# Moving split projection matmuls to later chunks, and the instruction-page edge by 8 instructions

## Chip, cores and metric

One core of a Trainium2 chip runs the whole program. The metric is the device time of one execution in microseconds (us). Times of single instructions are in nanoseconds (ns) where that is said.

## What is computed

The reference runs two blocks, twice each in turn, on x of 2048 tokens by 512 channels, with a layer norm before each and a residual added after each:

```python
for s in range(n_seg):                       # 64 segments of 32 tokens
    h = concat([mem, xs])                    # 8 memory tokens + 32 tokens
    q, k, v = h @ Wq, h @ Wk, h @ Wv         # 32 heads of 128
    p = softmax(mask(q k^T * scale))
    o = (p v) @ Wo                           # back to 512 channels
    mem = o[:, :M]                           # the next segment's memory
    outs.append(o[:, M:])
```

That is block A, a recurrence: the first 8 output rows of a segment are the memory of the next. Block B projects with w_in, applies gelu, normalises one half, multiplies it by the 2048 x 2048 matrix w_sp, gates the other half with it and projects with w_out. It has no recurrence.

## The kernel before, in words

`a_block` (L479) runs block A, `b_block` (L227) block B; the program is A, B, A, B. All weights of A stay in SBUF. In A the loop at L837 goes over 64 segments and calls `segment` (L681). PE, VectorE and ScalarE get their instructions in the order in which the code writes them (`tc.manual_schedule`), so the order in `segment` is the order on TensorE.

A segment's work on TensorE, in order:
- `qk(0)`, `qk(2)`, `qk(1)`, `qk(3)` (L695): the projections q0, k0, q1, k1, each for 16 heads, into `psm`. They need `hA`, the segment's 32 rows transposed, which `build_hA` (L651) makes once the output pass of the segment before has given the new memory.
- `scores(0)` (L712), then `v_mm(0)` (L705, the value projection v0 into `psV`), a `fill()`, `scores(1)`, `v_mm(1)` (v1), a `fill()`.
- the sums psM (L785), `pv` (L737), the sums psD (L791), a `fill()`.
- the output pass `wo_pass` (L595) into `pw`: 32 heads times 4 column groups, 128 matmuls of 128 columns, and a last `fill()`.

A fill takes the next piece of `more`, a generator. For s % 4 of 1 to 3 it is `b_units` (L570), the projections of the last 8 tokens of all segments of the next block of 128 tokens, which don't depend on the recurrence; for s % 4 == 0 from the fifth block of 128 on it is `y_part` (L615), a quarter of the outputs of those tokens.

Each projection of a segment is a chunk made by `mm_chunk` (L530): 4 k-steps times 4 column groups, 16 matmuls of 512 columns with 32 stationary columns each. With `halved=n`, n of the 16 are split into two matmuls of 256 columns each, which compute the same. Every matmul is two instructions on TensorE, a weight load and the matmul, so each split adds two instructions.

What the splits are for is seen in the constants. `PE_PAGE` is 256 instructions. `fills_of(s)` (L663) gives the number of instructions in each of a segment's four fills, SEGMENT_PE (600) what the rest of a segment has, and `pads_of(s)` (L671) the number n of splits that bring the distance from one output pass to the next to 3 x 256 instructions, and how they are dealt out to the chunks. So a multiple of 256 instructions lies at the same place in every segment of a block. `FILL_AHEAD` (L29) stands for the fills ahead of the first segment, one entry for each of the two runs of block A; it enters n of segment 0 alone, and so sets where that place is.

The chunks' splits before, from `pads_of` (each chunk has 16 at most):

| segments | n | q0 | k0 | q1 | k1 | v0 | v1 |
|---|---|---|---|---|---|---|---|
| 0 of the first A, of the second A | 35, 37 | 0 | 0 | 16 | 16 | 3, 5 | 0 |
| s % 4 == 0 or 1, s < 16 (not 0) | 68 | 4 | 16 | 16 | 16 | 16 | 0 |
| s % 4 == 0 or 1, 16 to 60 | 64 | 0 | 16 | 16 | 16 | 16 | 0 |
| s % 4 == 2 or 3, to 59 | 52 | 0 | 4 | 16 | 16 | 16 | 0 |
| 61 | 80 | 16 | 16 | 16 | 16 | 16 | 0 |
| 62, 63 | 84 | 16 | 16 | 16 | 16 | 16 | 4 |

Of the kernel before, what the change touches and what calls it, by code (L numbers as in the profile page):

```python
# [25 lines left out]
LN_EXP_SET = 6  # L26
PE_PAGE = 256
SEGMENT_PE = 600
FILL_AHEAD = ((0, 0, 0, 98), (0, 0, 0, 94))  # L29
FCH = [(0, 128), (128, 128), (256, 128), (384, 128), (512, 128), (640, 48)]  # L30
ORDERED = {mybir.EngineType.PE, mybir.EngineType.DVE, mybir.EngineType.Activation}

# [446 lines left out]
def a_block(tc, c, rows, front, MV_in, RS_in, MV_out, RS_out, wqkv, Wo, S, first):  # L479
# [6 lines left out]
    with ExitStack() as ctx:  # L486
# [176 lines left out]
        def fills_of(s):  # L663

            if s < 0:
                return FILL_AHEAD[not first]
            if s % 4 == 0:
                return (2, 2, 4, 8) if s // 4 > 3 else (0, 0, 0, 0)
            return (8, 8, 16, 32) if s // 4 + 1 < NB else (0, 0, 0, 0)

        def pads_of(s):  # L671

            n = (3 * PE_PAGE - SEGMENT_PE - fills_of(s - 1)[3] - sum(fills_of(s)[:3]) + 1) // 2
            pads = {}
            for chunk in ("q1", "k1", "v0", "k0", "q0", "v1"):
                pads[chunk] = min(n, 16)
                n -= pads[chunk]
            assert n == 0
            return pads

        def segment(s, fill, spare1, spare2, tail):  # L681
            tb, j4 = s // 4, s % 4
            pads = pads_of(s)
            st = seg_state.pop(s)
            QQ, KTB, VB = st["QQ"], st["KTB"], st["VB"]
# [239 lines left out]
```

## Time and profile before

| | before |
|---|---|
| median of 6 executions | 1861.03 us |
| lowest to highest | 1854.25 to 1865.81 us |
| the profiled execution, its own time | 1859.94 us |
| its span in the profile | 1858.2 us |
| TensorE matmuls busy | 1758.0 us, 51180 of them |
| weight loads busy | 1225.7 us, 51180 |
| VectorE busy | 1155.1 us |
| ScalarE busy | 1112.2 us |
| matmuls psm with Wk, at L544 | 281.1 us, 7440 of them, mean 285 ns |
| matmuls psV with Wv, at L544 | 274.1 us, 6136, mean 310 ns |
| matmuls pw at L599 | 258.8 us, 16640, mean 220 ns |
| mean granted TensorE clock | 0.988 |

The page gives busy time and share of the span for each engine, then DMA queues, then the chain: from the last instruction back, at each step to what released it. "Issue" in the chain is time in which an engine waited for nothing that the profile shows. A mean time of one matmul is the time that it is in the array's pipe, not the time that it adds[...]. What a chunk adds is read from start to start in the timeline. In a row of the chain of waits stand the start and the length in us, then the engine, the written tile, the line and the number of instructions merged.

### The profile page before, as it was taken

To read this page: it belongs to the slowest core of one execution; us is meant where nothing else is said; L and a number is where in the kernel's file an instruction comes from. 1 tells how busy PE (TensorE), PEld (TensorE's weight loads), DVE (VectorE), ACT (ScalarE), POOL (GpSimd) and SP (SyncE) were. 2 spreads that over 40 slices of the span, in tenths; PEclk is the share of its full clock that TensorE was granted. 3 is DMA by queue.
4 is the path that set the end of the run, shared out by engine and by line. 5 is a ranking of instruction groups with operands and counts; after the bars stand their busy time and mean duration, and the time that the engine had idled before them with its cause. 6 is when DMAs were issued, how large, how long until landed. Compare 5 with 4: busy or idle time off the path is not lost.

```text
span 1858.2 us, 109480 instructions
## 1 busy us (share of the span) xinstructions
PE 1758.0 (95%) x51180; PEld 1225.7 (66%) x51180; DVE 1155.1 (62%) x2700; ACT 1112.2 (60%) x2074; POOL 136.7 (7%) x289
## 2 busy tenths in 40 slices
PE   2999999999999999888989999999999999998898
PEld 1677777777777777645547777776677767765455
DVE  1666666676667766583346666666766676665722
ACT  1667766777777676571037767666677666665500
POOL 5000000000000000122010000000000000002000
PEclk8999999999999999999989999999999999999999
DMA  9100000021002111359840000001200120124585
GB/s 348 51 19 21 19 21 19 21 74 38 19 19 81 35 31 34 100 144 182 197 125 22 23 22 23 23 22 44 81 25 22 49 84 26 35 62 145 113 177 131
DMA packets 189327, 126.78 MB, mean 68 GB/s; under 512 B 135896, under 2 KB 164328, under 8 KB 188872
## 3 DMA queue, kind: packets, MB, share of 16 engines
q1 hardware_dynamic: 167016, 71.01, 16.2%
q0 software_dynamic: 10560, 34.07, 5.6%
q10 hardware_dynamic: 11296, 14.70, 2.6%
q8 instruction: 400, 6.55, 1.5%
q14 instruction: 55, 0.45, 0.1%
HBM read 59.29 MB, written 33.56 MB: 50 GB/s over the span
## 4 chain that ended last, share of the span: by engine, by line
PE 88%; DVE 4%; DMA 4%; ACT 2%; issue 2%; POOL 0%; SPq 0%; ACTq 0%; DVEq 0%; POOLq 0%
PE psm L544 25%; PE psV L544 13%; PE pw L599 12%; PE psb L544 10%; PE pg L332 7%; PE psS L720 5%; PE psO L743 4%; PE pwB L611 4%; PE py L360 3%; PE psD L795 2%; PE pz L266 2%; PE psM L785 1%; DMA Wk_sb<-in_A_Wk_dram 1%; DMA uT<-u 1%; PE psM L786 1%
## 5 line engine op out<-in xcount | busy, mean ns | idle before, releaser
L544 PEld LDWEIGHTS <-hA 128*32 128x32 bf16 x19872 | 521.4, 96 | 173.1 <-DVE hA L655 51.3
L699 ACT CAST rows<-psm 128x512 bf16<-128x512 f32 x512 | 300.1, 586 | 211.9 <-PE psm L544 211.9
L544 PE MATMUL psm<-Wk_sb,hA 128*32 128x256 bf16 (+1 forms) x7440 | 281.1, 285 | 8.8 <-issue 8.0
L544 PE MATMUL psm<-Wq_sb,hA 128*32 128x256 bf16 (+1 forms) x6296 | 275.9, 307 | 11.1 <-DVE hA L655 9.8
L544 PE MATMUL psV<-Wv_sb,hA 128*32 128x256 bf16 (+1 forms) x6136 | 274.1, 310 | 2.4 <-issue 2.4
L599 PEld LDWEIGHTS <-uT 128*32 128x32 bf16 x16640 | 234.4, 97 | 54.7 <-DVE uT L805 47.8
L599 PE MATMUL pw<-Wo_sb,uT 128*32 128x128 bf16 x16640 | 258.8, 220 | 11.6 <-DVE uT L805 6.7
L703 DVE STREAM_TRANSPOSE QQ<-rows 128x512 bf16<-128x512 bf16 x256 | 182.1, 711 | 77.3 <-ACT rows L699 76.2
L703 DVE STREAM_TRANSPOSE KA<-rows 128x512 bf16<-128x512 bf16 x256 | 181.9, 711 | 58.3 <-ACT rows L699 58.3
L724 ACT ACTIVATE E<-psS 128x448 bf16<-128x448 f32 x256 | 140.0, 547 | 127.8 <-PE psS L720 127.8
L755 DVE TENSOR_TENSOR uT<-psO,Rt 128x384 bf16<-128x384 f32 x256 | 138.6, 541 | 119.6 <-ACT Rt L811 119.4
L805 DVE TENSOR_TENSOR uT<-psO,Rm 128x128 bf16<-128x128 f32 x256 | 62.6, 286 | 164.6 <-PE psD L795 164.6
L811 ACT ACTIVATE Rt<-Rt 128x512 f32<-128x512 f32 x256 | 157.6, 629 | 4.1
L332 PE MATMUL pg<-z2n,wspT 128*128 128x344 bf16 x1024 | 156.5, 311 | 1.0 <-DVE u L340 1.0
L332 PEld LDWEIGHTS <-wspT 128*128 128x128 bf16 x1024 | 98.5, 98 | 55.6 <-issue 8.2
L803 ACT ACTIVATE Rt<-psD 128x1024 f32<-128x1024 f32 x128 | 131.2, 1025 | 5.9
L544 PEld LDWEIGHTS <-hB 128*32 128x32 bf16 x3072 | 77.6, 97 | 78.2 <-DVE hB L559 24.4
L720 PEld LDWEIGHTS <-KA 128*64 128x64 bf16 x2048 | 80.3, 113 | 68.0 <-DVE KA L703 34.8
L727 DVE TENSOR_TENSOR E<-E,maskN 128x448 bf16<-128x448 bf16 x256 | 95.3, 372 | 47.9 <-ACT E L724 47.9
L544 PE MATMUL psb<-Wq_sb,hB 128*32 128x512 bf16 x1024 | 90.1, 389 | 25.5 <-DVE hB L559 25.5
L720 PE MATMUL psS<-QQ,KA 128*64 128x80 bf16 x2048 | 111.9, 208 | 0.7 <-issue 0.3
L780 ACT CAST VA<-psV 128x512 bf16<-128x512 f32 x128 | 75.1, 586 | 56.6 <-PE psV L544 56.6
(147 smaller groups left out, 2226.0 us busy)
## 6 DMA issues: line engine op xcount, KB each, us to landing
Wo_sb<-in_A_Wo_dram POOLq DMA_DIRECT2D x8, 1024.0 KB, 13.3
xs<-xd ACTq DMA_DIRECT2D x32, 256.0 KB
o_d<-o_sb SPq DMA_DIRECT2D x126, 64.0 KB
y_o<-o_d SPq DMA_DIRECT2D x24, 256.0 KB
xd<-y_o SPq DMA_DIRECT2D x22, 256.0 KB
Wq_sb<-in_A_Wq_dram POOLq DMA_DIRECT2D x8, 512.0 KB, 6.9
Wk_sb<-in_A_Wk_dram POOLq DMA_DIRECT2D x8, 512.0 KB, 11.0
Wv_sb<-in_A_Wv_dram POOLq DMA_DIRECT2D x8, 512.0 KB, 11.2
```

The source lines that it names most:

```text
L332: nc.tensor.matmul(pg[t][:, k, 0:344], lhsT=wsp[t][:, st, :], rhs=z2n[:, st, 344 * k:344 * k + 344], start=(st == 0), stop=(st == NT - 1))
L544: nc.tensor.matmul(o, lhsT=lhs(kt, cg), rhs=r, start=(kt == 0 and a == 0), stop=(kt == KT - 1 or halved > 0), tile_position=(0, 32 * cg), ...
L599: nc.tensor.matmul(po[32 * cg:32 * cg + 32, 0:128], lhsT=lhs[:, n, :], rhs=wo_rhs(h, cg), start=(h == 0), stop=(h == H - 1), tile_position ...
L699: nc.scalar.copy(r[:], ps[:])
L703: nc.vector.transpose(out=QQ[:, j % 2, :, 0:32] if j < 2 else KA[:, j % 2], in_=r[:])
L720: nc.tensor.matmul(pS[64 * g:64 * g + 64, i, c0:80 if K is KA else 112], lhsT=K[:, r, n:n + 2, :].rearrange("p h k -> p (h k)"), rhs=q if ...
L724: nc.scalar.activation(out=E[:, r], in_=pS, func=ACT.Exp, scale=scale)
L727: nc.vector.tensor_tensor(out=E[:, r], in0=E[:, r], in1=maskN[:, j4, :].unsqueeze(1).to_broadcast([P, 4, 112]), op=ALU.mult)
L755: nc.vector.tensor_tensor(out=hview(uT_nxt[:], r, 8, 32), in0=oview(r, 8, 32), in1=Rr[:, :, :, 0:24], op=ALU.mult)
L780: nc.scalar.copy(VA[:, 1].rearrange("p i e -> p (i e)"), psV[1][:, 0, :])
L803: nc.scalar.activation(out=Rt[:], in_=psD[:], func=ACT.Ln)
L811: nc.scalar.activation(out=rt, in_=rt, func=ACT.Exp, scale=-1.0)
```

## The change

Two edits. The first entry of `FILL_AHEAD` goes from 98 to 106, so n of segment 0 in the first A is 31 in place of 35: 8 instructions fewer ahead of everything that follows. And `pads_of` deals the splits out by another list: v0 and k1 first, then v1 (16 for s % 4 == 0, else 8), q1 up to 12, k0 up to 8, and what is left to q1, v1, k0, q0.

```diff
-FILL_AHEAD = ((0, 0, 0, 98), (0, 0, 0, 94))
+FILL_AHEAD = ((0, 0, 0, 106), (0, 0, 0, 94))
...
-            pads = {}
-            for chunk in ("q1", "k1", "v0", "k0", "q0", "v1"):
-                pads[chunk] = min(n, 16)
-                n -= pads[chunk]
+            pads = dict.fromkeys(("q0", "k0", "q1", "k1", "v0", "v1"), 0)
+            for chunk, most in (("v0", 16), ("k1", 16), ("v1", 16 if s % 4 == 0 else 8), ("q1", 12), ("k0", 8), ("q1", 16), ("v1", 16),
+                                ("k0", 16), ("q0", 16)):
+                k = min(n, most - pads[chunk])
+                pads[chunk] += k
+                n -= k
             assert n == 0
             return pads
```

The splits after:

| segments | n | q0 | k0 | q1 | k1 | v0 | v1 |
|---|---|---|---|---|---|---|---|
| 0 of the first A | 31 | 0 | 0 | 0 | 15 | 16 | 0 |
| 0 of the second A | 37 | 0 | 0 | 0 | 16 | 16 | 5 |
| s % 4 == 0, s < 16 (not 0) | 68 | 0 | 8 | 12 | 16 | 16 | 16 |
| s % 4 == 1, s < 16 | 68 | 0 | 8 | 16 | 16 | 16 | 12 |
| s % 4 == 0, 16 to 60 | 64 | 0 | 4 | 12 | 16 | 16 | 16 |
| s % 4 == 1, 16 to 57 | 64 | 0 | 8 | 16 | 16 | 16 | 8 |
| s % 4 == 2 or 3, to 59 | 52 | 0 | 0 | 12 | 16 | 16 | 8 |
| 61 | 80 | 0 | 16 | 16 | 16 | 16 | 16 |
| 62, 63 | 84 | 4 | 16 | 16 | 16 | 16 | 16 |

The total of TensorE's matmuls goes from 51180 to 51176. The other engines and the queues keep their instructions in the same order. The second run of A begins 8 instructions earlier too, so the place of the multiples of 256 moves by 8 instructions in both runs of A: in the output pass, from 96 to 104 instructions after its start in the first A.

## The prediction

> **What bounds the kernel now.** I read the page first.
>
> ```profile
> PE 1758.0 (95%) x51180; PEld 1225.7 (66%) x51180; DVE 1155.1 (62%) x2700; ACT 1112.2 (60%) x2074; POOL 136.7 (7%) x289
> ...
> q8 instruction: 400, 6.55, 1.5%
> ...
> PE 88%; DVE 4%; DMA 4%; ACT 2%; issue 2%; POOL 0%; SPq 0%; ACTq 0%; DVEq 0%; POOLq 0%
> ```
>
> TensorE is the bound: 95% busy and 88% of the chain. The reader is to see two smaller things. Queue q8 carries instructions: 6.55 MB in 400 packets is 16 KB each, and 102,360 PE records (matmuls and weight loads) over 400 is 256 records for each packet. So one packet is one page, and PE_PAGE in the code is its length. 1.5% of 16 engines over 1858.2 us, shared by 400, is 1.11 us for each packet. And 2% of the chain is "issue", time in which PE waited for nothing that the profile shows. Summed over the chain of waits in the six stretches that hold the segments (63 to 780 and 976 to 1708 us), issue is some 21 us. That is about all that a better place for page edges can win.
>
> Next, the chain of waits in a segment with s % 4 == 0 (s = 16 of block 0), from its output pass on:
>
> ```profile
> 223.99 1.80 PE pw L599 x128
> 225.79 0.96 PE psb L544 x16
> 226.75 1.31 PE psm L544 x32
> 228.06 0.33 issue
> 228.39 2.40 PE psm L544 x80
> ...
> 235.82 1.90 PE pw L599 x128
> ```
>
> and TensorE's timeline of the same place:
>
> ```profile
> 226.56 1.05 PE L544 MATMUL psm<-Wq_sb,hA 128*32 128x512 bf16 x16
> 227.43 0.62 PE L544 MATMUL psm<-Wk_sb,hA 128*32 128x256 bf16 x16
> 228.39 0.63 PE L544 MATMUL psm<-Wk_sb,hA 128*32 128x256 bf16 x16 [0.33 <-issue]
> ```
>
> The stall falls inside k0, after 16 of its 32 halves. Nothing in the computation separates those two halves. Counted in instructions (a weight load and a matmul each): 256 of Wo, 32 of fill, 32 of q0, 32 of k0 is 352 = 96 + 256. The segment's other edges lie at 96 and 608. In block 1 the same edge comes one matmul earlier. Its Wo edge shows when pages are late:
>
> ```profile
> 1306.94 0.68 PE pw L599 x47
> 1307.62 0.08 issue
> 1307.70 1.33 PE pw L599 x81
> ...
> 1315.43 0.04 issue
> ...
> 1322.79 0.72 issue
> 1323.50 2.45 PE psm L544 x81
> ```
>
> From 1307.70 to 1323.50 four pages pass in 15.80 us, 3.95 us each, although work alone would take less. So there is a **fetch loop**: while transfers load the engines, a page can't follow the page before in less than 3.9 to 4.0 us. Where the chain shows no issue (the segment from 258.37 to 269.52 us, 11.15 us for three pages), the loop fits in 3.72 us. The kernel runs at the edge of it.
>
> [...] a split is nearly free. Here v0 with 32 halves takes 1.00 us in the chain, v1 with 16 whole ones 0.98.
>
> **The change, part by part.** *Added and removed instructions.* The number of splits is unchanged but for the first segment (35 to 31 in block 0), so 8 instructions fewer: 4 x 0.02/16 us, nothing. Chunks now get 8 or 12 splits, which no row shows. The rows with 4 (k0, 20 matmuls) and 16 start 0.87 and 0.88 us before the next chunk, and bracket them: cost 0. If the two halves of one column group held up the other groups, each k-step would lose 0.11 us, 0.4 us a chunk; 16 splits would then show it worst, and they don't. VectorE, ScalarE, GpSimd and the DMA queues keep their instructions in order; chunks end at the same time, so no evacuation moves.
>
> *The moved edges and splits.* A split chunk spends 13.8 ns on an instruction, a whole one 27, Wo 7. So moving splits changes how long a page lasts. From the on-time chain of a main segment with s % 4 == 0 (1364.85 to 1376.12: Wo 1.80, fill 0.95, q0, k0, q1, k1 3.51 together, scores 0.37, v0 1.00, pwB 0.32, scores 0.37, v1 0.98, pwB 0.32, psM 0.23, pv 0.59, psD 0.29, pwB 0.54):
> - before, pages from 96, 352 and 608: 160/256 x 1.80 + 0.95 + 0.87 + 0.44 = 3.38; then 0.44 + 0.88 + 0.89 + 0.37 + 1.00 = 3.58; then the rest and 96 of Wo, 4.31.
> - after (q0 0, k0 4, q1 12, k1, v0 and v1 16 splits; edges at 104, 360, 616): 1.07 + 0.95 + 0.87 + 0.87 = 3.76; then 0.88 + 0.89 + 0.37 + 1.00 + 0.32 + 0.37 + 0.09 = 3.92; then 3.59.
>
> [...] The timeline's starts of the output pass say what such segments really lose: the 22 main ones take 11.79 us on average and 11.37 at best, 9.1 us in sum; the six early ones 11.57 and 11.14, 2.6 us. So up to 0.4 us a segment could go. [...] I keep half: 22 x 0.2 = 4.4 and 1.3 for the early ones.
>
> *The other segments.* s % 4 of 2 and 3: 3.64, 3.70, 3.81 by the same count from the chain of 258.37; after 3.88, 3.76, 3.51. The sum of 11.15 is under three late loops either way, so they lose the same in busy stretches; I put 0. s % 4 == 1 is similar (third page about 3.4). The last four segments of a block have no fills and are filled with 80 to 84 splits, now with q0 nearly free of them instead of v1: their pieces of issue come to some 6 us, of which I take 0.8.
>
> Sum: 4.4 + 1.3 + 0.8 = 6.5 us. The profiled execution took 1859.94 us (span 1858.2 and 1.7 around it), so 1853.4; it lies 1.1 under the median of 1861.03, and against that median I say **1854.5**. The bounds: nothing (the loop alone decides) and all of 9.1 + 2.6 + about 1.3 = 13 us (1848).
>
> **The rivals.**
> 1. *The loop itself is the bound.* A stall in the busy stretch from 1307.70 is 3L whatever the pages hold. For it: late pages come in runs; against it: issue sits in the s % 4 == 0 segments far more than in the 22 of each of the other kinds (9.1 us lost against 1.8, 2.3 and 4.5 for s % 4 of 1, 2 and 3, counted in the same way). Then only the quiet ones gain, about 1 to 2 us: 1859.
> 2. *The full gain*[...]: 1848.
> 3. *Slower: the third page is now too short.* At 3.4 to 3.5 us instead of 3.7 to 3.8 [...] in the 96 or so segments with s % 4 of 1 to 3. [...] the Wo edge is late by 0.3 us there. It eats the gain of 6.5 us from 22 such stalls on, one segment in four to five; at one in two it costs 48 x 0.3 = 14, net 8 slower: 1869. [...]
> 4. *Unseen serialising in chunks of 8 and 12 splits* would cost far more (0.4 us in some 200 chunks, 80 us), and the chunks of 4 and 16 speak against it.
>
> **How the numbers follow.** Forecast (3 to 9 us won) 0.50; rival 1 0.27; rival 2 0.10; rival 3 0.10; rival 4 0.03. A measurement can tell about 0.3%, 5.6 us, from no change. So faster takes rival 2 and four fifths of the forecast, 0.50; same the rest of the forecast, rival 1 and a fifth of rival 3, 0.39; slower 0.11. The range: 1848 (all of it) to 1863 (rival 1 with the spread of the runs shown, 1854 to 1866, behind it); what is left out is the greater part of rivals 3 and 4.
>
> **What would show it.** Right: in the chain, no issue piece inside k0 of s % 4 == 0 segments, output passes there 11.4 us apart in quiet stretches; in the timeline the k0 chunk with 20 matmuls; q8 again 400 packets. Wrong: pieces of issue inside pw after 52 matmuls, in segments with s % 4 of 1 to 3 (rival 3), or v1 and q1 over 0.95 us from start to next start (rival 4), or the same issue total with its pieces at other places (rival 1).

## The result

| | before | after |
|---|---|---|
| median | 1861.67 us (40 runs, 1853.42 to 1872.82) | 1852.38 us (19 runs, 1844.85 to 1858.59) |
| after over before, 95% interval | | 0.9946 (0.9931 to 0.9960) |
| profiled execution, its own time | 1859.94 us | 1856.67 us |
| its span | 1858.2 us | 1854.9 us |

The change makes the kernel 0.54% faster, with an interval of 0.40 to 0.69%: some 10 us (7 to 13), where 6.5 were forecast. The profiled execution of after is one of its slower ones, so totals are taken from the timed runs, and the profile is used for places.

The page of after, its lines of engines, instruction queue and chain:

```profile
PE 1754.4 (95%) x51176; PEld 1246.3 (67%) x51176; DVE 1156.2 (62%) x2700; ACT 1111.5 (60%) x2074; POOL 136.7 (7%) x289
...
q8 instruction: 400, 6.55, 1.5%
...
PE 86%; DVE 5%; DMA 4%; ACT 2%; issue 2%; POOL 0%; SPq 0%; ACTq 0%; POOLq 0%; DVEq 0%
```

Nothing in these says why one kernel is faster: nearly the same busy times, the same 400 packets, issue at 2% again. The difference is at the page edges. The chain of waits of after in the segment whose chain was shown of before (s = 16 of block 0; start, length, what):

```profile
223.43 1.88 PE pw L599 x128
225.32 0.87 PE psb L544 x16
226.19 1.80 PE psm L544 x24
227.99 0.36 issue
228.35 1.94 PE psm L544 x56
...
235.31 1.72 PE pw L599 x113
```

The stall is still there in this execution, but it has moved. TensorE's timeline shows that it now stands between k0 and q1, where the edge at 360 lies, and that k0 is a chunk of 20 matmuls:

```profile
226.94 1.05 PE L544 MATMUL psm<-Wk_sb,hA 128*32 128x512 bf16 x20
228.35 1.06 PE L544 MATMUL psm<-Wq_sb,hA 128*32 128x512 bf16 x28 [0.36 <-issue]
229.22 1.06 PE L544 MATMUL psm<-Wk_sb,hA 128*32 128x256 bf16 x32
```

So one segment proves little. The gain is in how many segments stall. The table takes each main segment's time from TensorE's timeline, start of one output pass (L599) to the next; a segment that loses nothing takes 11.37, 11.30, 11.15 and 11.15 us for s % 4 of 0, 1, 2 and 3. It has the mean of 22 segments for each kind and the sum of the last four segments of both runs of A. "Again" are the second profiles of both kernels, taken one after the other on one chip.

| profile | 0 | 1 | 2 | 3 | last four, both runs |
|---|---|---|---|---|---|
| before | 11.79 | 11.38 | 11.25 | 11.35 | 97.4 |
| before again | 11.67 | 11.37 | 11.28 | 11.26 | 98.9 |
| after | 11.56 | 11.46 | 11.31 | 11.33 | 97.1 |
| after again | 11.48 | 11.48 | 11.19 | 11.27 | 92.7 |

The same traces say where the time goes. An edge counts as late here when the first matmul behind it starts more than 0.05 us later after the matmul ahead of it than at the best edge of its kind. The first edge is the one in the output pass (96 instructions after its start in before, 104 in after), the second comes 256 instructions later, in k0 or just behind it, and the third another 256 later. The table has the number of late edges in the main segments and what they add up to; an output pass is counted with the segment that follows it.

| late edges | of | before | before again | after | after again |
|---|---|---|---|---|---|
| the second edge, s % 4 == 0 | 22 | 16, 6.8 us | 16, 4.6 us | 8, 3.0 us | 6, 2.0 us |
| the third edge, s % 4 == 0 | 22 | 7, 1.9 us | 8, 1.8 us | 1, 0.2 us | 0 |
| the first edge, all kinds | 88 | 6, 1.3 us | 3, 0.7 us | 24, 5.3 us | 7, 2.3 us |
| the second and third edge, the other kinds | 132 | 22, 5.8 us | 13, 3.6 us | 16, 1.8 us | 2, 0.4 us |

The late edges of the s % 4 == 0 segments sum to 9.0, 6.5, 4.3 and 2.5 us in the four profiles, and that is all that these segments lose against 11.37 us each. The change takes away the late third edge and about half of the lateness at the second, and more edges are late in the output pass.

That these stalls are waits for instructions can be read from the packets on q8, each of which the trace has with its start and end. In before, all 29 stalls of more than 0.15 us at the first and second edge of main segments end 1.24 to 1.61 us after a packet has landed. The packet of the stall at 228.39 us landed at 226.89, that of the stall at 1323.50 at 1322.04.

A pair of chains from those second profiles, of the same segment (s = 36 of block 0), shows the difference of the two deals. Before:

```profile
449.85 1.80 PE pw L599 x128
451.64 0.96 PE psb L544 x16
452.60 1.31 PE psm L544 x32
453.91 0.20 issue
454.11 2.40 PE psm L544 x80
...
461.55 1.45 PE pw L599 x94
```

After:

```profile
448.27 1.80 PE pw L599 x128
450.08 0.95 PE psb L544 x16
451.03 3.49 PE psm L544 x80
...
459.54 1.90 PE pw L599 x128
```

From output pass to output pass it is 11.70 against 11.27 us; with the edge behind k0 and k0 nearly whole, the 1.31 + 0.20 + 2.40 us of the projections become 3.49. The stall costs more than its piece of issue: the first row behind it is 0.2 us longer than the 2.21 us that its chunks take by the prediction's count.

### The profile page after: what moved, and what is told of

It reads as the page before. It is cut to its first block, busy times and chain, and to the rows that moved or that the text cites. A ratio compares the mean times of both kernels' runs of the same rounds, so it can differ in the third digit from the quotient of the medians.

```text
span 1854.9 us, 109472 instructions
## 1 busy us (share of the span) xinstructions
PE 1754.4 (95%) x51176; PEld 1246.3 (67%) x51176; DVE 1156.2 (62%) x2700; ACT 1111.5 (60%) x2074; POOL 136.7 (7%) x289
## 4 chain that ended last, share of the span: by engine, by line
PE 86%; DVE 5%; DMA 4%; ACT 2%; issue 2%; POOL 0%; SPq 0%; ACTq 0%; POOLq 0%; DVEq 0%
PE psm L544 25%; PE psV L544 13%; PE pw L599 12%; PE psb L544 10%; PE pg L332 7%; PE psS L722 5%; PE psO L745 4%; PE pwB L611 3%; PE py L360 3%; PE psD L797 2%; PE psM L787 1%; DMA uT<-u 1%; DMA Wk_sb<-in_A_Wk_dram 1%; PE pz L266 1%; PE psM L788 1%
## 5 line engine op out<-in xcount | busy, mean ns | idle before, releaser
L544 PEld LDWEIGHTS <-hA 128*32 128x32 bf16 x19868 | 542.4, 96 | 171.7 <-DVE hA L655 51.9
L599 PE MATMUL pw<-Wo_sb,uT 128*32 128x128 bf16 x16640 | 263.4, 220 | 16.0 <-DVE uT L807 8.9
L544 PE MATMUL psm<-Wk_sb,hA 128*32 128x256 bf16 (+1 forms) x6623 | 276.1, 299 | 2.5 <-issue 1.7
L599 PEld LDWEIGHTS <-uT 128*32 128x32 bf16 x16640 | 235.8, 97 | 62.6 <-DVE uT L807 50.2
L544 PE MATMUL psV<-Wv_sb,hA 128*32 128x256 bf16 x7477 | 275.3, 284 | 0.9 <-issue 0.9
L544 PEld LDWEIGHTS <-hB 128*32 128x32 bf16 x3072 | 88.8, 98 | 68.0 <-DVE hB L559 24.8
L544 PE MATMUL psb<-Wq_sb,hB 128*32 128x512 bf16 x1024 | 93.9, 397 | 25.9 <-DVE hB L559 25.9
```

The source lines that it names most:

```text
L544: nc.tensor.matmul(o, lhsT=lhs(kt, cg), rhs=r, start=(kt == 0 and a == 0), stop=(kt == KT - 1 or halved > 0), tile_position=(0, 32 * cg), ...
L599: nc.tensor.matmul(po[32 * cg:32 * cg + 32, 0:128], lhsT=lhs[:, n, :], rhs=wo_rhs(h, cg), start=(h == 0), stop=(h == H - 1), tile_position ...
```

## The experiments

Twelve runs were made in three groups, each group on a chip of its own. The chips differ (before has medians of 1850, 1860 and 1849 us in the three), so ratios are compared, each to before on the same chip. A gain in us is the ratio's, times the median of before. The theory is the one of the prediction: pages of 256 instructions against a fetch loop. The rivals keep their numbers; segment times are each from one profile.

**The new deal alone.** The splits as after, the edges as before.

```diff
-FILL_AHEAD = ((0, 0, 0, 106), (0, 0, 0, 94))
+FILL_AHEAD = ((0, 0, 0, 98), (0, 0, 0, 94))
```

> The new dealing of the splits with the old first entry of FILL_AHEAD (98), so the page edges stay at 96, 352 and 608 instructions after the start of the output pass. Theory (page lengths against the fetch loop): most of the gain is here, since it is the dealing that brings the first page of an s % 4 == 0 segment from 3.4 to about 3.8 us: 7 us under before, some 1854.5. Rival 1 (the loop decides whatever the pages hold): no gain beyond 1 to 2 us, 1860. Rival 3 (third page too short): its share is here too, so then this run is slower than the whole change by some us.

0.9964 (0.9952 to 0.9976), 6.7 us of 1850. That is the theory's size, and over rival 1's 1 to 2 us. That it is some us slower than the whole change, as rival 3 has it, is not excluded: the change's 0.9946, from another chip, has an interval that overlaps. The s % 4 == 0 segments take 11.44 us.

**The moved edge alone.** The kernel before with 106 for 98.

> The old dealing with FILL_AHEAD 106 alone: every page edge 8 instructions later, chunks as before. Theory: the first page of an s % 4 == 0 segment gives up 8 instructions of Wo (0.06 us) and takes 8 of k0 (0.11 us), a tenth of what the whole change does to it: 2 us under before, 1859.5, within the noise. Rival: the place of the edge in the output pass is what counts, not the lengths: then nearly the whole 9 us are here, 1853.

0.9969 (0.9955 to 0.9984), 5.7 us (3 to 8), where the theory expected 2 and the rival nearly 9: neither was right. What follows was worked out afterwards. The expectation looked only at the first page. At 608 the third edge lies ahead of the first pwB matmul of an s % 4 == 0 segment, at 616 behind it. So the second page gains 0.32 us of pwB and 0.07 of the scores and gives up 0.11 of k0. The first two pages together then hold 3.43 + 3.86 = 7.29 us, where they held 6.96. Eight instructions are much when one of them, a pwB matmul, adds 0.32 us. In the trace the third edge of these segments is late in none of 22, where before had 7 and 8. The two halves of the change bring 6.7 and 5.7 us, the whole some 10; whether they add up or each lifts the same limit, these intervals don't tell.

**New deal for s % 4 == 0 only, and for the others only.** Edges as after in both; the edit is a condition around the two lists in `pads_of`.

```diff
+            if s % 4 == 0:
                 pads = dict.fromkeys(("q0", "k0", "q1", "k1", "v0", "v1"), 0)
...
+            else:
+                pads = {}
```

> New dealing for s % 4 == 0 alone, old for the other segments; edges as in the changed kernel. Theory: nearly all of the gain, since only there were the pages uneven (3.38, 3.58, 4.31 us by the sum): 6 to 9 us under before, 1853 to 1855. Rival 3 (the third page of 3.5 us in s % 4 of 1 to 3 costs something): faster than the whole change, by 2 us or more.

> New dealing for s % 4 of 1 to 3, old for s % 4 == 0; edges as in the changed kernel. Theory: the pages of those were even before, so little more than the moved edge gives: 2 to 4 us under before, 1858 to 1860. Rival 1 in the form that any segment gains alike: three quarters of the gain, 7 us, 1854.5. Rival 3: slower than before.

Only s % 4 == 0: 0.9953 (0.9938 to 0.9968), 8.7 us. Only the others: 0.9981 (0.9969 to 0.9992), 3.5 us, no more than the edge alone. Both are what the theory expected; rival 1's 7 us in the second and rival 3's slower kernel there are not seen, and the first is not faster than the whole change. So the new deal brings more in a quarter of the segments than in the other three quarters, where these intervals show no gain from it. How much it adds to the moved edge in that quarter stays open: 8.7 and 5.7 us have overlapping intervals. Between the two kernels the segments say the same: those of s % 4 == 0 take 11.47 us in the first kernel and 11.76 in the second. A late one of the second, with k0 still split, in the chain of waits:

```profile
1266.50 0.74 PE pw L599 x51
1267.23 0.13 issue
1267.36 1.28 PE pw L599 x77
1268.64 0.86 PE psb L544 x16
1269.50 1.56 PE psm L544 x35
1271.06 1.14 issue
1272.20 2.37 PE psm L544 x77
```

The edges stand 4 matmuls (8 instructions) later than in before, at pw 51 and inside k0, and both are late: the first page takes 4.84 us from 1267.36 to 1272.20 for 3.7 us of work. This segment follows one of s % 4 == 3 whose third page is now 3.5 us, and it starts late already. Most of the 1.14 us is a longer loop, though: the packet of the next page starts 2.12 us after 1267.36, where 1.16 is the middle value behind late edges in the kernel of the next experiment, and data keep the DMA engines 57% busy in between.

**The loop by itself.** All chunks fully split, so that there are more pages than the loop can deliver.

```diff
-            assert n == 0
-            return pads
+            return dict.fromkeys(pads, 16)
```

> All 16 matmuls of every projection chunk in two halves: 111,807 TensorE instructions where the changed kernel has 102,391, the same arithmetic. A page then holds less than 3.5 us of work nearly everywhere, so the fetch loop binds and its period is measured directly. Theory: about 437 pages; those of block A at 3.7 to 3.8 us each, some 100 to 130 us slower than before, 1960 to 1990. If a split only costs its fixed time (0.02 us for 16): 5 us slower. If the stalls are something other than instruction pages, the same 5 us.

1.0583 (1.0549 to 1.0616), 109 us slower with the same arithmetic and 36 packets more on q8, as the theory had it. The page's queue line, and the chain over four pages:

```profile
q8 instruction: 436, 7.14, 1.5%
```

```profile
273.26 1.41 PE pw L599 x99
274.67 1.13 issue
275.80 0.62 PE pw L599 x29
276.42 0.86 PE psb L544 x16
...
288.54 1.09 PE psm L544 x39
289.63 0.36 issue
289.99 2.68 PE psm L544 x89
```

Between the two places there are 1024 instructions, four pages, in 289.99 - 275.80 = 14.19 us. That is 3.55 us a page. The loop can be taken apart in this trace, by the middle values of 134 stalls of more than 0.35 us: a packet takes 1.03 us, TensorE goes on 1.39 us after its end, and the next packet starts 1.16 us after that, 3.58 us together. Over all main segments four kinds take 12.77 + 11.80 + 12.46 + 12.42 us by the timeline and hold 3376 instructions, 13.2 pages: 3.75 us a page. In before and after a page has 11.15 to 11.37 us over three, 3.72 to 3.79. The kernel sits on the loop's mean, so a page that holds less work than that can be late.

**No splits.** The same edit with 0 for 16.

> No matmul split: 87,231 TensorE instructions, pages drift through the segment. Theory: on average a page has 4.3 us of work, over the loop, but one that covers the output pass and pv has 3 us or less, and each of those stalls: about 10 us slower than before, 1872, with pieces of issue wherever an edge follows the output pass. Rival (what costs is the number of pages or instructions): 59 pages fewer, so faster than both, by 20 us or more.

1.0067 (1.0045 to 1.0089), 12.5 us slower with 60 fewer packets (340), near the theory's 10. The number of pages alone isn't the cost: then it would be faster. An edge that stalls late in the output pass, in its chain:

```profile
410.60 1.58 PE pw L599 x111
412.18 1.12 issue
413.30 0.45 PE pw L599 x17
```

**Edges 64 instructions earlier.** After, with 42 for 106.

> The changed kernel with the first entry of FILL_AHEAD at 42: all page edges 64 instructions earlier, at 40, 296 and 552 after the start of the output pass, the dealing as in the change. Theory: the first page then holds 216 instructions of Wo, 1.5 us, with fill and a quarter of q0, 2.7 us in all in segments with a full fill, 1 us under the loop[...]: slower than before, by 10 us or more, 1870 to 1880. Rival 1 (only the loop counts, three pages are three pages): the same as the changed kernel, 1853.

1.0260 (1.0233 to 1.0286), 48 us slower: the direction of the theory, but far over its 10 to 20 us. Rival 1, in which only the loop counts, falls: the pages are as many as in after. The timeline has the stall behind the fourth matmul of q0, at 296:

```profile
266.07 0.40 PE L544 MATMUL psm<-Wq_sb,hA 128*32 128x512 bf16 x4
266.88 0.83 PE L544 MATMUL psm<-Wq_sb,hA 128*32 128x512 bf16 x12 [0.41 <-issue]
```

By a count made afterwards the first page has 216/256 x 1.80 + 0.95 + 0.21 = 2.68 us of work in three quarters of the segments, 1.07 under the 3.75 of the loop. They take 12.26, 11.97 and 11.90 us for s % 4 of 0, 2 and 3, 0.89, 0.82 and 0.75 over the times without loss.

**A shorter third page.** After, with up to 16 splits in v1 of every segment.

```diff
-            for chunk, most in (("v0", 16), ("k1", 16), ("v1", 16 if s % 4 == 0 else 8), ("q1", 12), ...
+            for chunk, most in (("v0", 16), ("k1", 16), ("v1", 16), ("q1", 12), ...
```

> The changed kernel with up to 16 splits in v1 of every segment, taken from q1 (4 left where n is 52). It lengthens the first page of s % 4 of 2 and 3 and shortens the third further, to about 3.2 to 3.3 us. Theory: nothing much, within 2 us of the changed kernel[...]. Rival 3 (a short third page stalls at the Wo edge): in 60 segments 0.2 us or more beyond the change, 12 us slower than it, 1864.

0.9962 (0.9947 to 0.9976). Against the change's 0.9946 that is 3 us, with overlapping intervals and on another chip: not rival 3's 12, and no proof of the theory's 2.

**Both kernels again**, for profiles on one chip with those of the next two.

> The kernel before once more, for a profile taken beside those of the runs with it. Theory: in the 22 main segments with s % 4 == 0 the first matmul behind the edge in k0 starts 0.2 us or more late on average, and the segments take 11.7 to 11.8 us. Rival (the first profile was an unlucky execution): under 0.1 us and 11.5.

> The changed kernel once more, for a profile beside the one of before. Theory: the s % 4 == 0 segments 0.2 us or more shorter than in before, the others within 0.05 us of it on average. Rival 3: the others longer by 0.1 us or more, with the lateness at the edge in the output pass.

Single executions of 1852.31 and 1840.69 us. The s % 4 == 0 segments went from 11.67 to 11.48, those of 1 from 11.37 to 11.48, of 2 from 11.28 to 11.19, of 3 from 11.26 to 11.27. In before the edge in k0 is 0.21 us late on average, as expected, and its segments are just under the 11.7 to 11.8 of the theory; the rival's 0.1 and 11.5 are not seen. In after the gain of 0.19 is just short of the 0.2 expected, and the other kinds change by 0.01 on average, though s % 4 == 1 alone by 0.11.

**Later edges.** New deal for s % 4 == 0 alone with FILL_AHEAD 122 (edges at 120, 376 and 632); and the old deal with 138.

> New dealing for s % 4 == 0 alone, and every edge 16 instructions later than in the changed kernel (FILL_AHEAD 122). Theory: both even the pages out further, but the loop allows little more: 6 to 10 us under before, within 3 us of the changed kernel. Rival (the place of the edge decides, and 104 is its best): slower than the changed kernel by 3 us or more.

> The old dealing with every edge 40 instructions later than before (FILL_AHEAD 138): 136, 392 and 648 after the start of the output pass. The first page of s % 4 == 0 then holds 120 of Wo, the fill, q0, all of k0 and 8 of q1, 3.8 us, with no chunk dealt otherwise. Theory (it is page lengths that count, by whatever means): as fast as the changed kernel, 6 us under before or more. Rival (what counts is that the split chunk isn't just ahead of or on an edge): no gain, since the edge now falls in the split q1.

0.9916 (0.9896 to 0.9935) and 0.9890 (0.9869 to 0.9911): 15.5 and 20.3 us under before. The first gains well over the 6 to 10 us that were expected, so that forecast missed. The second beats the change clear of both intervals, the first all but so (0.9935 against 0.9931). The best version, 1829.78 us where before has 1849.38, is the old kernel with one number changed, edges at 136, 392 and 648. The rival that wanted the split chunk away from the edge falls: the edge lies in the split q1 there. In the first the s % 4 == 0 segments reach 11.37, the time without loss. In the second they keep 11.56, but the others go to 11.30, 11.15 and 11.24, the last four segments to 92.9 us, and the second A's time from its first output pass to its second from 16.75 to 11.27. So not all of the 20 us is evener pages in the main segments: against before again its profile is 22.5 us shorter, of which the main segments have 6.9, the last four 6.0 and that one place 5.5, and block B behind the second A is 2.9 shorter.

## Why the prediction was right, point by point

*The sum.* The time lies in the range, in the direction forecast, and the mechanism is the one forecast. The gain is larger than the sum of 6.5 us, which lies under the measured 7 to 13. Of its terms some held and some did not, so that the sum came near is in part luck.

*Page edges against a fetch loop.* Shown. Stalls at page edges end 1.24 to 1.61 us after a packet has landed; more pages with the same work cost 109 us, the same pages 64 instructions earlier 48, and fewer pages don't make it faster. In the kernel with all chunks split, a packet follows the one before by 3.76 us on average in the main segments. The prediction had "3.9 to 4.0" under load and "fits in 3.72" without. Load does less than that: with under 5% of the DMA engines busy with data the mean is 3.74, with 20 to 50% it is 3.82.

*Is the sequencer ahead of the array at an edge?* The packets say so in direction only. In before, the next packet starts 1.14 us after the second edge of a main segment where the first matmul behind it starts over 0.15 us after the one ahead of it (24 edges, middle value), but 0.87 us after it where that gap is under 0.05 us (32 edges). If a packet is asked for when the sequencer reaches the edge, then at the edges on time it was 0.27 us further ahead of the array, an estimate from these two values. How far ahead it can be, no run here shows.

*The s % 4 == 0 segments, 4.4 us.* Measured in these segments: 4.9 in one pair of profiles, 4.1 in the other. Halving the bare gain was the author's estimate. Part of it does come back in the output passes: 5.3 us of late edges against 1.3, and 2.3 against 0.7. But in the segments with s % 4 == 0 most of what is still lost is behind k0 (3.0 and 2.0 us), though by the count the page that ends there holds 3.76 us and the one that ends in the output pass 3.59; why is open. In sum the late edges of the main segments fall by 5.5 us in the first pair and by 6.0 in the second.

*The early ones, 1.3 us.* 0.4 and 1.7 us in the two pairs.

*The other kinds, 0.* For s % 4 of 2 and 3 together the pairs say 0.8 us longer and 1.8 shorter, so no sign. But s % 4 == 1 grew by 1.6 and 2.4 us, and not by page edges: 1.6 us of it in each pair is waiting just ahead of an output pass, in one or two segments. The chain of waits of after at s = 29 of the first A:

```profile
374.96 4.53 DMA o_d<-yB
379.49 0.02 issue
379.51 3.76 DMA y_o<-o_d
...
383.90 0.29 DVE uT L807
384.19 0.04 issue
384.24 1.97 PE pw L599 x128
```

VectorE waits for the load of `y_o` and makes `uT` for the pass after it. The prediction had no such term. Before again has such a wait of 1.05 us, too, at s = 45 of the second A, so whether the change brings it on is not shown.

*The last four segments, 0.8 us.* This term of the sum was mis-sized, as far as single executions tell: they gained 0.3 us in the first pair of profiles and 6.2 in the second. Nor do all four lack fills, as the prediction says: s = 60 has them. How much the term is worth on average stays open: these eight segments differ by 1.5 us between the two profiles of before and by 4.4 between those of after.

*Rival 1, the loop alone,* falls with the experiments that move edges: three pages are three pages, yet 48 us lie between two places of the edge. *Rival 2, the full gain,* does not hold: the s % 4 == 0 segments keep 11.56 and 11.48 us, over 11.37. *Rival 3, the third page too short,* has its mechanism: 24 of 88 output passes in after have a late edge, 7 in the second profile, where before has 6 and 3. It does not have its price, a slower kernel: a late edge there costs 0.2 to 0.3 us, and fewer are late at the other edges. A short page alone does not make an edge late: in the kernel with edges at 136, 392 and 648 the third page of s % 4 == 2 has 0.25 + 0.21 + 0.33 + 0.59 + 0.28 + 0.55 + 0.96 = 3.17 us of work, under every loop seen, and those segments take 11.15 us, no loss. What covers it there is not shown. *Rival 4*, whose 0.4 us a chunk is an estimate, half of the 0.87 us of a chunk, fell: in the second profile of after, chunks with 8 and 12 splits start 0.86 to 0.87 us before what follows (middle values), and q1 with 28 matmuls starts 0.87 us before k1 in the timeline above (228.35 to 229.22). That a split costs next to nothing rests on these rows and on those of v0 and v1 (1.00 and 0.98 us).

## What to carry to other kernels

When TensorE executes very many short instructions, look at the instruction queue's packets, divide the instructions by them, and count where the page edges fall. A page that holds less work than the fetch loop takes, here 3.75 us, can be late, so place the edges such that slow instructions spread over all pages. Here 256 instructions of the output pass take 1.80 us, half of the loop, and an edge that leaves 216 of them in one page cost 48 us. Before dealing work out anew, try the edges at several places with a few instructions ahead of the loop: of the places tried here, one was worth twice the change.

## What was not expected of the hardware

An instruction packet came late during a load of data. In before, when the second A begins and Wo (4 MB) is loaded, the DMA view of 955 to 963 us has the software queue at 101.6% of the engines, and only two instruction packets:

```profile
q0 software_dynamic: 710, 2.78, 101.6%
q8 instruction: 2, 0.03, 1.7%
```

and the chain stops at the page edge in the first output pass there:

```profile
961.97 0.85 PE pw L599 x47
962.82 2.55 issue
965.37 1.78 PE pw L599 x81
```

TensorE waited for nothing that the profile shows and stood for 2.55 us, in the middle of an output pass. It went on 1.53 us after a packet had landed. That packet had started at 962.74, 4.2 us after the edge before it was passed (958.53), where 1.16 is the middle value behind late edges in the kernel with all chunks split. In the second profiles the time from this pass to the next was 16.75 us in before, 16.44 in after, and 11.27 with the edges 40 instructions later. There the chain has 1.55 us of issue in v1 ahead of that first pass, and the stretch from the first A's last segment to that pass is 1.0 us longer, so part of the stall only moved. That the load delays the fetch is read from these views; a kernel with the load at another time was not tried.
